# Attention with head mixing and a two-matrix MLP on one core: MLP products in runs of four, w_in spread over 48 steps, and both half-precision copies of e on ScalarE

## The chip, the cores and the metric

The kernel runs on one core of a Trainium2 chip. The metric is device time in microseconds, the median of three runs; the kernel before takes 851.1 us (850.71 to 854.3). The rows below come from one profiled execution, which took 852.55 us and whose span from the first to the last instruction is 850.8 us.

## The reference

Four batches, twelve heads, 448 positions, 64 channels per head. The scores are mixed across heads before the softmax, the probabilities are mixed across heads after it, and an MLP with a clipped gate follows:

```
scores = scale * q @ k.T                       # (4, 12, 448, 448)
scores = einsum('bhij,hg->bgij', scores, w_pre)
attn   = exp(scores - max) / sum
attn   = einsum('bhij,hg->bgij', attn, w_post)
x      = (attn @ v) as (1792 tokens, 768)
h      = x @ w_in                               # (1792, 2048), w_in is float64
out    = (h * clip(h + 3, 0, 6) / 6) @ w_out    # (1792, 768), w_out is float64
```

## The kernel before, in words

**Attention.** Each batch is cut into four chunks of query rows (120, 120, 120 and 90). For a chunk TensorE makes the scores of twelve heads in six products of two heads (L370). They go into the one two-bank PSUM tile `pair`, ScalarE copies them out (L402, tile `s`) and a DMA writes them to a scratch tensor `sd` in DRAM. When a whole chunk is in the scratch, it is read back in another layout, heads and ten query rows on the partitions: that is the load `T_all<-sd` (L453). One load serves two steps of ten rows each, called a step pair here; a batch has 45 steps and the whole attention 92 step pairs. Of each step pair TensorE mixes the heads (L461), VectorE takes the row maximum (L468), ScalarE the exponential `e` with its sum (L469), GpSimd multiplies with the reciprocal sum (L477). From step 24 on, `e` is split into two half-precision parts: `eh`, a rounded copy, and `el`, the rest, which GpSimd subtracts (L483). The copy of the first half of the step pair is made by ScalarE (L482), that of the second half by VectorE (L480). TensorE then mixes the heads again (L499) into `A`, which ScalarE and VectorE copy out of PSUM (L510, L508). After a chunk TensorE multiplies `A` with `v` (L536) into `x`.

**MLP, first part.** Two chunks make a group G of 240 or 208 tokens; there are eight groups. `moe1(G, fcs)` makes 18 matrix products for each of the 16 pieces `fc` of w_in (L694), in one PSUM bank each, ScalarE forms the gate (L703, tile `rl`), VectorE the product (L705, tile `g`, two pieces in one tile, two tiles in a ring), and a DMA writes two pieces to DRAM (L708). A piece of 18 products is called an MLP product below.

**w_in.** Each of its 16 pieces (786 KB of float64) is loaded (L622), decoded by ScalarE and VectorE (L582 to L597), scaled and split in two half-precision parts (L640 to L647). Two pieces are loaded before the first T load, the next six with steps 0, 2, ... 10, the last eight with steps 20, 23, ... 41. Groups that are ready before step 44 do their first eight pieces first; the other eight wait until step 44.

**MLP, second part.** The same with w_out, from 628 us to the end (L883).

**Order.** All operations are first put in a list with a modelled duration, dependencies and a priority (class `Plan`). `Plan.run` then walks through time and writes each engine's order out; TensorE takes the ready operation with the best priority, but stays with the kind of operation that it did last (`mode`) where one of that kind has a priority within `STAY`. MLP products have the worst priorities (5000 and more) and fill TensorE when nothing of the attention is ready in the model. In model gaps a `filler` puts products that no result needs (L729). All DMAs are issued by SP, in the order of the list. On the chip each engine runs its list in order and waits where the model was too early.

Of the kernel before, what the change touches and what calls it, by code (L numbers as in the profile page):

```python
# [42 lines left out]
LEAD = 7  # L43
HALF, W_AT, EARLY, V_AT = 8, 20, 2, 2
POST16 = 24
# [5 lines left out]
class Op:  # L51
    __slots__ = ("eng", "dur", "fn", "prio", "n", "succ", "order", "ready", "end", "bytes", "no", "mode", "takes")

# [48 lines left out]
class Plan:  # L102

    DMA_RATE = 330e3
    HOP = 0.14
# [7 lines left out]
    def op(self, eng, dur, fn, r=(), w=(), prio=0.0, after=(), nbytes=0, mode=0):  # L115
        o = Op()
        o.eng, o.dur, o.fn, o.prio, o.bytes, o.mode = eng, dur, fn, prio, nbytes, mode
        o.succ, o.order, o.n, o.ready, o.no, o.end, o.takes = [], [], 0, 0.0, len(self.ops), None, []
        deps = {}
# [30 lines left out]
    def run(self):  # L150
# [9 lines left out]
        free, wait, ready, out = {}, {}, {}, []  # L160
        bw, mode = 0.0, None

# [27 lines left out]
        while True:  # L190
# [19 lines left out]
            if e == "PE":  # L210
                at = [(avail(x[2]), x) for x in ready[e]]
                at = [x for z, x in at if z is not None and z <= t + 1e-9]
                x = min(at)
                x = min([z for z in at if z[2].mode == mode and z[0] < x[0] + self.STAY] or [x])
                ready[e].remove(x)
                o = x[2]
                for b in o.takes:
                    b.pool.take(b, self.HOP)
            else:
                while wait[e] and wait[e][0][0] <= t + 1e-9:  # L220
                    o = heapq.heappop(wait[e])[2]
                    heapq.heappush(ready[e], (o.prio, o.no, o))
                o = heapq.heappop(ready[e])[2]
# [24 lines left out]
def body(ctx: ExitStack, tc: tile.TileContext, q4, kT, vj, wpre0, wpost0, ident0, w_in, w_out, outT):  # L248
# [107 lines left out]

    def queries(b, c, at):
        t = buf(rot, [P, 6, CI], F32, "qx", f"qx_{b}_{c}", 2)
        qs[b, c] = t
        dma(P * 2880, lambda: SP.dma_start(t(), q4[b, c]), [], [t], at)  # L360

# [12 lines left out]
    def first_scores(pr, at):  # L374
# [8 lines left out]
        pe(0.73, products(q, k, pr, at2), [(k, pr % 3), q], ps, at, mode=1)  # L383
        h = 2 * pr
# [7 lines left out]
    def scores(b, c, pr, at):  # L392
# [6 lines left out]
        ps = place(pairs)  # L399
        pe(0.73, products(q, k, pr, [lambda u=u: ps()[:, u, :S] for u in range(2)]), [(k, pr % 3), q], [ps], at, mode=1)  # L400
        st = buf(rot, [CI, 2, S], F32, "s", f"s_{b}_{c}_{pr}", 2)
# [37 lines left out]
    def step(s):  # L439
# [24 lines left out]
        e = buf(rot, [P, 2, S], F32, "e", f"e_{s}", 3)  # L464
        pe(0.37 * R, pre, [T, wpre8], [*ps, (e, "pe")], s - 0.7, mode=1)
        eh, el = (buf(rot, [P, 2, S], F16, x, f"{x}_{s}", 2) if s >= POST16 else None for x in ("eh", "el"))
# [9 lines left out]
        for r in range(R):  # L476
            pool(0.63, lambda r=r: POOL.tensor_scalar(e()[:, r], e()[:, r], rr()[:, r:r + 1], 1.0, op0=ALU.mult, op1=ALU.mult), [rr], [(e, r)], s + 0.6 + 0.3 * r)  # L477
            if s >= POST16:
                if r:
                    dve(0.35, lambda: DVE.tensor_copy(eh()[:, 1], e()[:, 1]), [(e, 1)], [(eh, 1)], s + 0.95)  # L480
                else:
                    act(0.47, lambda: ACT.activation(eh()[:, 0], e()[:, 0], AF.Copy), [(e, 0)], [(eh, 0)], s + 0.65)  # L482
                pool(1.02, lambda r=r: POOL.tensor_tensor(el()[:, r], e()[:, r], eh()[:, r], op=ALU.subtract), [(e, r), (eh, r)], [(el, r)], s + 0.7 + 0.3 * r)  # L483
        if s < POST16:
            mix, dur = [(e, wpost_n)], 1.05
        else:
            mix, dur = [(eh, wpost_h), (eh, wpost_l), (el, wpost_h)], 0.4
        po = [place(mixed) for u in range(2)]
# [124 lines left out]
    def w_in_item(fc, after=()):  # L613
# [3 lines left out]
        w = wi_g[g]  # L617
        at = (fc - 4 if fc < EARLY else 2 * fc if fc < HALF else W_AT + 3 * (fc - HALF)) + 8
        raw = buf(rot, [P, NCC * P], I64, "stw", f"wi_{fc}", 2)
        o = buf(rot, [P, DM], F32, "wf", f"wf_i{fc}", 3)  # L620
        st, am1, t, r = (buf(rot, [P, 1], F32, f"wi_{x}", f"wi{x}_{fc}", 4) for x in ("st", "am", "t", "r"))
        dma(786432, lambda: SP.dma_start(raw(), w_in[fc]), [], [raw], at, after)  # L622
        rest = decode(raw, o, DM, (st, st), at, (0.81, 0.94, 0.48, 0.89, 0.89))
        slot, top = across(st, f"wi{fc}", at + 0.15)
        rest()
        p = (pwi, fc)

        dve(1.1, lambda: pow64(top, am1, t, lambda: pwi()[:, fc:fc + 1], r), [(slot, 1)], [am1, t, p, r], at + 0.2)

# [48 lines left out]
    def moe1(G, fcs):  # L678
# [7 lines left out]
        for fc in fcs:  # L686
# [16 lines left out]
            act(0.44, lambda fc=fc, pv=pv, r=r: ACT.activation(r()[:, :n], pv(), AF.Relu, bias=three()[:, fc:fc + 1], scale=uh()[:, fc:fc + 1]),  # L703
                [ps, (three, fc), (uh, fc)], [r], -80)
            dve(0.37, lambda fc=fc, pv=pv, r=r, gt=gt: DVE.scalar_tensor_tensor(gt()[:, fc % 2, :n], r()[:, :n], six()[:, fc:fc + 1], pv(),  # L705
                                                                                op0=ALU.min, op1=ALU.mult), [r, ps, (six, fc)], [(gt, fc % 2)], -80)
            if fc % 2:
# [7 lines left out]
    pool(2.0, lambda: POOL.memset(T_all()[:4], 0.0), [], [T_all], -20)  # L715
    warm = wpool.tile([P, 512], F16, tag="g", name="warm", bufs=2)
    DVE.memset(warm, 0.0)
# [31 lines left out]
    held, scales = [], []  # L749
# [194 lines left out]
```

## Time and profile before

| | |
|---|---|
| median of three runs | 851.1 us (850.71 to 854.3) |
| profiled execution, its own time | 852.55 us |
| its span | 850.8 us |
| TensorE busy | 816.4 us (96%) |
| VectorE, ScalarE, GpSimd busy | 547.1, 505.3, 371.6 us |
| mean granted TensorE clock | 0.984 |
| DMA | 177.09 MB, 208 GB/s over the span |

The busy share of TensorE is an average over very different stages: the start (to about 100 us), the attention with MLP products in between (to 547 us), the rest of the first MLP part (to 628 us) and the second MLP part. A row of a table of stretches gives its bounds and length in us, then busy time and number of instructions of each engine, then the granted clock, the busy share of the DMA engines and GB/s.

### The profile page before, as it was taken

The page shows a single profiled execution, that of the slowest core. Times are in us where ns is not written, and L with a number is a line of the kernel's source. Part 1 is how long each engine was busy: PE and PEld are TensorE (multiplying, and loading weights), DVE is VectorE, ACT ScalarE, POOL GpSimd, SP SyncE. Part 2 cuts the span into 40 slices and gives each one's busy share as a digit, 9 for nine tenths or more (in the row PEclk, how much of TensorE's full clock was granted, in tenths as well). Part 3 has the DMA queues.
Part 4 walks back from the last instruction along what each step waited for, and adds up shares of the span by engine and source line. Part 5 has one row for each costly group of instructions (what it writes and reads, how often), then busy time and mean ns, then how long its engine had stood idle before and what let it go on. Part 6 is the DMA issues. An engine that isn't in the chain of part 4 may idle for free.

```text
span 850.8 us, 25699 instructions
## 1 busy us (share of the span) xinstructions
PE 816.4 (96%) x10722; PEld 553.8 (65%) x10722; DVE 547.1 (64%) x1137; ACT 505.3 (59%) x969; POOL 371.6 (44%) x550
## 2 busy tenths in 40 slices
PE   8889998899999989999999999999999999999998
PEld 2456666567777656766766888999975555555554
DVE  5579799998667687876886665762228885333330
ACT  4547778678777867787667565753335454334330
POOL 1335879988868757877658656000000000000000
PEclk9969799999999999999999999999999999999999
DMA  9988978788697997987887622852247775545530
GB/s 317 308 254 264 288 237 261 216 243 249 193 255 220 280 286 239 278 262 234 247 262 231 202 76 80 248 183 69 67 143 222 245 216 156 175 145 163 160 121 33
DMA packets 82872, 177.09 MB, mean 208 GB/s; under 512 B 7604, under 2 KB 51732, under 8 KB 82756
## 3 DMA queue, kind: packets, MB, share of 16 engines
q1 hardware_dynamic: 82756, 175.45, 67.2%
q8 instruction: 84, 1.38, 0.7%
q14 instruction: 32, 0.26, 0.1%
HBM read 113.38 MB, written 62.04 MB: 206 GB/s over the span
## 4 chain that ended last, share of the span: by engine, by line
PE 73%; DVE 8%; DMA 7%; POOL 6%; ACT 3%; issue 2%; SPq 0%; ACTq 0%; DVEq 0%; POOLq 0%
PE single L883 26%; PE single L694 22%; PE single L499 7%; PE single L536 6%; PE pair L370 6%; PE single L461 5%; DMA sd<-s 3%; POOL el L483 2%; POOL e L477 2%; DVE nb L468 2%; DMA T_all<-sd 2%; DMA wo<-in_w_out 1%; ACT e L469 1%; ACT s L402 1%; DMA v<-in_vj 1%
## 5 line engine op out<-in xcount | busy, mean ns | idle before, releaser
L694 PEld LDWEIGHTS <-wi 128*128 128x128 f16 x2304 | 211.4, 98 | 37.4 <-issue 30.3
L694 PE MATMUL single<-x,wi 128*128 128x208 f16 (+1 forms) x2304 | 234.2, 260 | 1.6 <-DVE g L705 1.0
L883 PE MATMUL single<-g,wo 128*128 128x448 f16 x1152 | 219.1, 353 | 0.0
L483 POOL TENSOR_TENSOR el<-e,eh 128x448 f16<-128x448 f32 x156 | 167.5, 1087 | 44.5 <-ACT eh L482 30.4
L883 PEld LDWEIGHTS <-wo 128*128 128x128 f16 x1152 | 112.2, 98 | 104.2
L469 ACT ACTIVATE e<-single,nb 128x448 f32<-128x448 f32 x180 | 112.7, 632 | 48.0 <-DVE nb L468 44.3
L477 POOL TENSOR_SCALAR e<-e,r 128x448 f32<-128x448 f32 x180 | 124.9, 705 | 25.6 <-DVE r L472 23.2
L870 DVE SCALAR_TENSOR_TENSOR g<-gr,gs,g 128x896 f16<-128x896 f32 x64 | 73.4, 1151 | 85.8 <-ACT g L869 85.6
L468 DVE TENSOR_REDUCE nb<-single 128x1 f32<-128x448 f32 x180 | 103.3, 612 | 15.9 <-PE single L461 15.6
L705 DVE SCALAR_TENSOR_TENSOR g<-rl,six,single 128x240 f32<-128x240 f32 (+1 forms) x128 | 56.7, 443 | 77.0 <-ACT rl L703 74.5
L703 ACT ACTIVATE rl<-single,three,uh 128x240 f32<-128x240 f32 (+1 forms) x128 | 68.7, 537 | 61.6 <-PE single L694 60.2
L869 ACT ACTIVATE g<-gr,gs 128x896 f16<-128x896 f32 x64 | 66.2, 1037 | 63.8 <-DMA gr<-gd 62.2
L370 PE MATMUL pair<-ks,qx 64*64 64x448 f32 (+1 forms) x736 | 94.3, 579 | 6.1 <-ACT s L402 5.3
L402 ACT ACTIVATE s<-pair 120x896 f32<-120x896 f32 (+1 forms) x90 | 82.4, 915 | 26.7 <-PE pair L370 13.4
L461 PE MATMUL single<-T_all,wpre 64*64 64x448 f32 (+1 forms) x720 | 89.2, 560 | 6.4 <-DMA T_all<-sd 6.4
L876 POOL TENSOR_TENSOR us<-gu,wo_p 128x1 f32<-128x1 f32 x24 | 6.7, 313 | 174.7 <-DVE wo_p L606 142.5
L536 PE MATMUL single<-A,v 128*64 128x120 f32 (+1 forms) x1536 | 77.4, 261 | 3.7 <-DVE A L508 1.7
L499 PEld LDWEIGHTS <-eh 60*128 60x128 f16 x2496 | 66.4, 100 | 21.7 <-issue 19.4
L536 PEld LDWEIGHTS single<-A,v 128*64 128x64 f32 x1536 | 74.3, 137 | 9.4 <-issue 3.1
L499 PE MATMUL single<-wpost_h,el 60*128 60x60 f16 x1248 | 73.6, 202 | 2.5 <-POOL el L483 2.5
L499 PE MATMUL single<-wpost_h,eh 60*128 60x60 f16 x1248 | 73.6, 202 | 2.3 <-DVE A L508 2.0
L499 PE MATMUL single<-wpost_l,eh 60*128 60x60 f16 x1248 | 73.4, 202 | 0.8 <-issue 0.8
(116 smaller groups left out, 890.6 us busy)
## 6 DMA issues: line engine op xcount, KB each, us to landing
T_all<-sd SPq DMA_DIRECT2D x88, 420.0 KB, 5.9
sd<-s SPq DMA_DIRECT2D x72, 420.0 KB, 5.7
gr<-gd SPq DMA_DIRECT2D x64, 448.0 KB, 3.7
wi<-in_w_in SPq DMA_DIRECT2D x16, 768.0 KB, 6.6
wo<-in_w_out SPq DMA_DIRECT2D x24, 512.0 KB, 5.1
gd<-g SPq DMA_DIRECT2D x32, 240.0 KB, 3.1
sd<-s SPq DMA_DIRECT2D x24, 315.0 KB, 4.8
gd<-g SPq DMA_DIRECT2D x32, 208.0 KB, 2.6
```

The costliest lines, as they stand in the source:

```text
L370: PE.matmul(at[u]()[c:c + m], q()[r, pr, c:c + m], k()[r, pr % 3, :], start=True, stop=True)
L402: act(0.82, lambda: ACT.activation(st()[:n], ps()[:n, :, :S], AF.Copy), [ps], [st], at + 0.5)
L461: PE.matmul(ps[r]()[64 * u:64 * u + 64, :S], wpre8()[rows], T_all()[rows, slot, u], start=True, stop=True)
L468: dve(0.53, lambda r=r: DVE.tensor_reduce(nb()[:, r:r + 1], ps[r]()[:, :S], axis=AX.X, op=ALU.max, negate=True), [ps[r]], [(nb, r)], s + 0 ...
L469: act(0.62, lambda r=r: ACT.activation(e()[:, r], ps[r]()[:, :S], AF.Exp, bias=nb()[:, r:r + 1], accum_out=sm()[:, r:r + 1]), [ps[r], (nb, ...
L477: pool(0.63, lambda r=r: POOL.tensor_scalar(e()[:, r], e()[:, r], rr()[:, r:r + 1], 1.0, op0=ALU.mult, op1=ALU.mult), [rr], [(e, r)], s + ...
L483: pool(1.02, lambda r=r: POOL.tensor_tensor(el()[:, r], e()[:, r], eh()[:, r], op=ALU.subtract), [(e, r), (eh, r)], [(el, r)], s + 0.7 + 0 ...
L499: PE.matmul(out, x()[rows, r, js], z()[rows], start=(i == 0), stop=(i == len(mix) - 1))
L536: PE.matmul(ps()[u * D:(u + 1) * D, k:k + n], v()[:, jc, g * D:(g + 1) * D], a()[:, jc * H + g, :n], start=(jc == 0), stop=(jc == NJ - 1))
L694: PE.matmul(pv(), wi_g[g]()[:, w, f0, cc, :], x()[:, z, cc, :n], start=(cc == 0 and i == 0), stop=(cc == 5 and i == 2))
L870: dve(1.1, lambda: DVE.scalar_tensor_tensor(g()[:, 1], raw(), sb(), g()[:, 0], op0=ALU.mult, op1=ALU.subtract), [raw, sb, (g, 0)], [(g, 1) ...
L883: PE.matmul(ps()[:, :S], two()[:, z, w, fc, :], gs[h, b, k]()[:, x, fc % 2, :], start=(fc == 0 and i == 0), stop=(fc == NFC - 1 and i == 2))
```

## The change

The first half of the edits concerns the list: `Op` gets a field `then`, and TensorE, where the operation that it did last names a successor that is ready, takes this one ahead of anything else. `moe1` links pieces so that runs of up to four MLP products come about (0 to 3, 4 to 7, and so on). The gate now overwrites the place of `g` in its tile, the tile `rl` is gone, and the ring of `g` has three tiles in place of two; in the list the MLP product waits for its `g` tile. The last eight pieces of w_in are loaded with steps 20, 26, ... 62 in place of 20, 23, ... 41, and the MLP products of held groups are added two pieces at a time. One piece in place of two is loaded ahead of the first T load. The queries of chunk 1 come after the first T load, and its scores have a lead of 5 steps in place of 7. Both `eh` copies are ScalarE's. Some modelled durations and the modelled DMA rate are changed.

```diff
-HALF, W_AT, EARLY, V_AT = 8, 20, 2, 2
+HALF, W_AT, W_BY, EARLY, V_AT = 8, 20, 6, 1, 2
-    DMA_RATE = 330e3
+    DMA_RATE = 345e3
-                x = min([z for z in at if z[2].mode == mode and z[0] < x[0] + self.STAY] or [x])
+                x = min([z for z in at if z[2] is then] or [z for z in at if z[2].mode == mode and z[0] < x[0] + self.STAY] or [x])
+                then = x[2].then
-    def queries(b, c, at):
+    def queries(b, c, at, after=()):
...
-                if r:
-                    dve(0.35, lambda: DVE.tensor_copy(eh()[:, 1], e()[:, 1]), [(e, 1)], [(eh, 1)], s + 0.95)
-                else:
-                    act(0.47, lambda: ACT.activation(eh()[:, 0], e()[:, 0], AF.Copy), [(e, 0)], [(eh, 0)], s + 0.65)
+                act(0.47, lambda r=r: ACT.activation(eh()[:, r], e()[:, r], AF.Copy), [(e, r)], [(eh, r)], s + 0.65 + 0.3 * r)
...
-        at = (fc - 4 if fc < EARLY else 2 * fc if fc < HALF else W_AT + 3 * (fc - HALF)) + 8
+        at = (fc - 4 if fc < EARLY else 2 * fc if fc < HALF else W_AT + W_BY * (fc - HALF)) + 8
...
-                gt = buf(wpool, [P, 2, 240], F32, "g", f"g_{G}_{fc}", 2)
-            r = buf(wpool, [P, 240], F32, "rl", f"rl_{G}_{fc}", 2)
+                gt = buf(wpool, [P, 2, 240], F32, "g", f"g_{G}_{fc}", 3)
+            r = lambda gt=gt, fc=fc: gt()[:, fc % 2, :n]
-            pe(0.0077 * n, mm, [x, (uh, fc), *[(wi_g[g], (k, fc)) for k in range(3)]], [ps], at + fc)
+            m1 = pe(0.00775 * n, mm, [x, (uh, fc), *[(wi_g[g], (k, fc)) for k in range(3)]],
+               [ps, (gt, ("pe", fc % 2))], at + fc)
+            if fc % 4 and fc > fcs[0]:
+                m0.then = m1
+            m0 = m1
...
-            todo.append((prev + (pr * n) / 6 - LEAD, 0, b, c, pr))
+            todo.append((prev + (pr * n) / 6 - (LEAD if C > 1 else 5), 0, b, c, pr))
...
+        if s < NS:
+            step(s)
         while todo and todo[0][0] - 2 <= s:
             at, _, b, c, pr = todo.pop(0)
+            C0 = 4 * b + c - 1
             if pr == 0:
-                queries(b, c, at - 5)
+                queries(b, c, at - 5, [t_load[0]] if C0 == 0 else [])
             scores(b, c, pr, at)
-        if s < NS:
-            step(s)
...
-        if s in range(W_AT, W_AT + 3 * (NFC - HALF), 3):
-            w_in_item(HALF + (s - W_AT) // 3, [t_load[s]])
-        if s == W_AT + 3 * (NFC - HALF):
-            for G in held:
-                moe1(G, range(HALF, NFC))
+        if s in range(W_AT, W_AT + W_BY * (NFC - HALF), W_BY):
+            fc = HALF + (s - W_AT) // W_BY
+            w_in_item(fc, [t_load[s]])
+            if fc % 2:
+                n_wi = fc + 1
+                for G in held:
+                    moe1(G, range(fc - 1, fc + 1))
...
-                    late = s < W_AT + 3 * (NFC - HALF)
-                    moe1(2 * b + c // 2, range(HALF if late else NFC))
-                    held.extend([2 * b + c // 2] * late)
+                    moe1(2 * b + c // 2, range(n_wi))
+                    if n_wi < NFC:
+                        held.append(2 * b + c // 2)
```

## Rows read from the trace of the kernel before

**Rows 1.** Span and mean granted TensorE clock of the core.
```profile
core 0: 850.8 us, clock 0.984
```

**Rows 2.** Stretches: bounds, length, PE, PEld, DVE, ACT, POOL busy, clock, DMA, GB/s.
```profile
24.00:48.00 24.00, 17.70 (x188) 9.18 (x186) 13.01 (x26) 12.96 (x29) 6.99 (x13) 1.00 0.95 310
48.00:62.00 14.00, 13.95 (x99) 8.62 (x99) 9.11 (x21) 7.96 (x14) 7.26 (x13) 0.51 0.83 243
62.00:100.00 38.00, 35.76 (x426) 23.71 (x424) 31.87 (x84) 28.85 (x55) 24.43 (x44) 0.87 0.84 265
100.00:200.00 100.00, 90.05 (x1519) 63.79 (x1518) 95.96 (x200) 77.51 (x152) 85.17 (x125) 1.00 0.81 242
200.00:420.00 220.00, 214.46 (x4218) 152.73 (x4219) 162.37 (x358) 166.47 (x368) 166.57 (x228) 1.00 0.83 250
...
440.00:547.00 107.00, 106.28 (x1910) 85.58 (x1909) 69.03 (x148) 69.37 (x152) 62.82 (x87) 1.00 0.56 166
547.00:628.00 81.00, 81.00 (x862) 79.07 (x861) 32.77 (x70) 33.74 (x60) 0.47 (x3) 1.00 0.36 114
628.00:848.00 220.00, 219.11 (x1157) 112.44 (x1155) 102.03 (x150) 86.11 (x105) 4.38 (x12) 1.00 0.54 167
```

**Rows 3.** ScalarE's eh copies (L482) by stretch, one for each step pair: busy, clock, DMA.
```profile
100.00:200.00 100.00, 8.64 (x15) 1.00 0.81 242
200.00:300.00 100.00, 12.70 (x22) 1.00 0.80 238
```

**Rows 4.** VectorE's groups of lines, 100 to 200 us: busy us, mean ns | idle before.
```profile
L597 DVE SCALAR_TENSOR_TENSOR wf_i<-wi,wf_i 128x768 int32<-128x768 int32 x8 | 11.1, 1382 | 0.1
L593 DVE SCALAR_TENSOR_TENSOR wf_i<-wi,wf_i 128x768 int32<-128x768 int32 x8 | 10.8, 1356 | 0.1
L480 DVE CAST eh<-e 128x448 f16<-128x448 f32 x14 | 9.8, 698 | 1.0 <-POOL e L477 0.9
```

**Rows 5.** The two eh copies, whole span: ns min/median/max, first and last start.
```profile
L480 DVE CAST eh<-e x76: 371/394/1221, 103.7 to 522.2; 128x448 f16<-128x448 f32 x76
...
L482 ACT ACTIVATE eh<-e x80: 559/577/607, 102.8 to 525.4; 128x448 f16<-128x448 f32 x80
```

**Rows 6.** Waits of all engines: us in total, times, longest us.
```profile
POOL el L483 <- ACT eh L482: 30.4, 40, 10.1
...
PE single L461 <- DMA T_all<-sd: 6.4, 3, 3.8
...
PE pair L370 <- ACT s L402: 5.3, 10, 1.5
...
PE single L499 <- POOL el L483: 2.5, 3, 1.0
```

**Rows 7.** Chain that ended last: start us, us, what.
```profile
34.77 13.14 DMA T_all<-sd
...
188.54 1.95 PE single L694 x18
191.40 3.80 PE single L694 x36
...
528.23 9.33 PE single L694 x90
...
556.44 71.36 PE single L694 x756
```

**Rows 8.** Timeline of TensorE, its first MLP product: start us, us.
```profile
111.88 2.00 PE L694 MATMUL single<-x,wi 128*128 128x240 f16 x18
```

**Rows 9.** DMA issues by SP at the start: start us, us of issuing.
```profile
5.91 1.26 SPq L622 DMA_DIRECT2D wi<-in_w_in  x2
...
10.63 0.40 SPq L403 DMA_DIRECT2D sd<-s  x1
...
16.37 4.60 SPq L403 DMA_DIRECT2D sd<-s  x2
24.84 1.31 SPq L453 DMA_DIRECT2D T_all<-sd  x3
```

More of the change, by code (lines that the diff above doesn't have):

```diff
@@ L51 @@
 class Op:
-    __slots__ = ("eng", "dur", "fn", "prio", "n", "succ", "order", "ready", "end", "bytes", "no", "mode", "takes")
+    __slots__ = ("eng", "dur", "fn", "prio", "n", "succ", "order", "ready", "end", "bytes", "no", "mode", "takes", "then")
 class Buf:
@@ L117, in op @@
         o.eng, o.dur, o.fn, o.prio, o.bytes, o.mode = eng, dur, fn, prio, nbytes, mode
-        o.succ, o.order, o.n, o.ready, o.no, o.end, o.takes = [], [], 0, 0.0, len(self.ops), None, []
+        o.succ, o.order, o.n, o.ready, o.no, o.end, o.takes, o.then = [], [], 0, 0.0, len(self.ops), None, [], None
         deps = {}
@@ L160, in run @@
         free, wait, ready, out = {}, {}, {}, []
-        bw, mode = 0.0, None
+        bw, mode, then = 0.0, None, None
         def push(o):
@@ L355, in keys @@
                     b * STEPS - 30 + 3 * j + i if b else -14 + 3 * j + i)
-    def queries(b, c, at):
+    def queries(b, c, at, after=()):
         t = buf(rot, [P, 6, CI], F32, "qx", f"qx_{b}_{c}", 2)
         qs[b, c] = t
-        dma(P * 2880, lambda: SP.dma_start(t(), q4[b, c]), [], [t], at)
+        dma(P * 2880, lambda: SP.dma_start(t(), q4[b, c]), [], [t], at, after)
     S0 = buf(apool, [CI, H, S], F32, "A", "s0", 2)
@@ L382, in first_scores @@
             at2 = [lambda u=u: two()[:, u, :S] for u in range(2)]
-        pe(0.73, products(q, k, pr, at2), [(k, pr % 3), q], ps, at, mode=1)
+        pe(0.77, products(q, k, pr, at2), [(k, pr % 3), q], ps, at, mode=1)
         h = 2 * pr
@@ L399, in scores @@
         ps = place(pairs)
-        pe(0.73, products(q, k, pr, [lambda u=u: ps()[:, u, :S] for u in range(2)]), [(k, pr % 3), q], [ps], at, mode=1)
+        pe(0.77, products(q, k, pr, [lambda u=u: ps()[:, u, :S] for u in range(2)]), [(k, pr % 3), q], [ps], at, mode=1)
         st = buf(rot, [CI, 2, S], F32, "s", f"s_{b}_{c}_{pr}", 2)
@@ L464, in step @@
         e = buf(rot, [P, 2, S], F32, "e", f"e_{s}", 3)
-        pe(0.37 * R, pre, [T, wpre8], [*ps, (e, "pe")], s - 0.7, mode=1)
+        pe(0.39 * R, pre, [T, wpre8], [*ps, (e, "pe")], s - 0.7, mode=1)
         eh, el = (buf(rot, [P, 2, S], F16, x, f"{x}_{s}", 2) if s >= POST16 else None for x in ("eh", "el"))
@@ L486, in step @@
         else:
-            mix, dur = [(eh, wpost_h), (eh, wpost_l), (el, wpost_h)], 0.4
+            mix, dur = [(eh, wpost_h), (eh, wpost_l), (el, wpost_h)], 0.44
         po = [place(mixed) for u in range(2)]
@@ L622, in w_in_item @@
         dma(786432, lambda: SP.dma_start(raw(), w_in[fc]), [], [raw], at, after)
-        rest = decode(raw, o, DM, (st, st), at, (0.81, 0.94, 0.48, 0.89, 0.89))
+        rest = decode(raw, o, DM, (st, st), at, (0.81, 0.94, 0.5, 1.15, 1.25))
         slot, top = across(st, f"wi{fc}", at + 0.15)
@@ L626, in w_in_item @@
         p = (pwi, fc)
-        dve(1.1, lambda: pow64(top, am1, t, lambda: pwi()[:, fc:fc + 1], r), [(slot, 1)], [am1, t, p, r], at + 0.2)
+        dve(1.2, lambda: pow64(top, am1, t, lambda: pwi()[:, fc:fc + 1], r), [(slot, 1)], [am1, t, p, r], at + 0.2)
         def m4():
@@ L697, in moe1 @@
             if fc % 2 == 0:
-                gt = buf(wpool, [P, 2, 240], F32, "g", f"g_{G}_{fc}", 2)
-            r = buf(wpool, [P, 240], F32, "rl", f"rl_{G}_{fc}", 2)
+                gt = buf(wpool, [P, 2, 240], F32, "g", f"g_{G}_{fc}", 3)
+            r = lambda gt=gt, fc=fc: gt()[:, fc % 2, :n]
             if gi == 0 and b == 0:
                 pool(0.25, lambda fc=fc: POOL.tensor_tensor(uh()[:, fc:fc + 1], pw2()[:, fc:fc + 1], u1(), op=ALU.mult), [(pw2, fc), u1], [(uh, fc)], -90)
-            pe(0.0077 * n, mm, [x, (uh, fc), *[(wi_g[g], (k, fc)) for k in range(3)]], [ps], at + fc)
[L703 to L706, printed above, removed]
+            m1 = pe(0.00775 * n, mm, [x, (uh, fc), *[(wi_g[g], (k, fc)) for k in range(3)]],
[3 more added lines that the diff above has]
+            m0 = m1
+            act(0.44, lambda fc=fc, pv=pv, r=r: ACT.activation(r(), pv(), AF.Relu, bias=three()[:, fc:fc + 1], scale=uh()[:, fc:fc + 1]),
+                [ps, (three, fc), (uh, fc)], [(gt, fc % 2)], -80)
+            dve(0.37, lambda fc=fc, pv=pv, r=r: DVE.scalar_tensor_tensor(r(), r(), six()[:, fc:fc + 1], pv(),
+                                                                                op0=ALU.min, op1=ALU.mult), [ps, (six, fc)], [(gt, fc % 2)], -80)
             if fc % 2:
@@ L715, in body @@
     pool(2.0, lambda: POOL.memset(T_all()[:4], 0.0), [], [T_all], -20)
-    warm = wpool.tile([P, 512], F16, tag="g", name="warm", bufs=2)
+    warm = wpool.tile([P, 512], F16, tag="g", name="warm", bufs=3)
     DVE.memset(warm, 0.0)
@@ L746, in body @@
         for pr in range(6):
-            todo.append((prev + (pr * n) / 6 - LEAD, 0, b, c, pr))
+            todo.append((prev + (pr * n) / 6 - (LEAD if C > 1 else 5), 0, b, c, pr))
     todo.sort()
-    held, scales = [], []
+    held, scales, n_wi = [], [], HALF
     for s in range(NS + 12):
```

## The prediction

> **What bounds the kernel now.** First the clock and the span [rows 1]: at 0.984 over 850.8 us about 13.6 us of the span are lost to TensorE's lower level. Then the table of stretches [rows 2]. From 547 us TensorE is busy to within 1 us of every stretch: 81 us of MLP products, then the second MLP part, 220 us. Nothing in the change shortens those products, so the end comes as early as TensorE gets through the rest of its work. Before 547 us it is idle 6.3 us in 24 to 48, 2.2 us in 62 to 100, 10 us in 100 to 200, and then 5.5 us in 220 (2.5 per 100). TensorE is therefore the bound from 200 us on, and the reader should see that another engine is it in 100 to 200: VectorE is busy 95.96 us of 100 there, against 74% in 200 to 420. The count of step pairs says the same: 15 in 100 to 200 and 22 in the next 100 us [rows 3]. VectorE's groups of lines of that stretch [rows 4] show what it does in excess: eight w_in pieces, of which two lines alone take 21.9 us, and the casts of eh with 9.8 us.
>
> At the start the DMA engines are the bound: share 0.95 at 310 GB/s in 24 to 48 [rows 2], and a T load issued at 34.77 lands 13.14 us later [rows 7]. TensorE's wait for T loads is 6.4 us in all, 3.8 us at the longest [rows 6]. Right behind that landing, from 48 to 62 us, the granted clock is 0.51, the level of 1.2 GHz [rows 2]; 0.49 x 14 = 6.9 us go there, and 0.13 x 38 = 4.9 us in 62 to 100.
>
> The sum goes against the profiled execution, 852.55 us (span 850.8 and 1.75 around it); it is 1.45 us above the median 851.1, which is taken off at the end.
>
> **Runs of four.** A single MLP product of 240 tokens costs 1.95 us of the chain, two in a row 3.80, five in a row 9.33 [rows 7]: a run costs 0.10 us more than its products. Between the first, at 111.88 [rows 8], and the last run of 42 products (x756 at 556.44 [rows 7]) TensorE's timeline has, the first counted, 68 runs with 86 products, 56 of them of one. With links of up to four, and the two held groups in smaller bits, groups 0 and 1 make 11 runs and the other 54 products 13 or 14: some 43 runs fewer. Each missing run also joins what stood on its two sides, which the trace does not price by itself; the nearest rows are again the 0.10 us of a run, so one saving of 0.10 is the lower end (4.3 us) and three of it the upper (13 us). I take 0.14, near the priced row: **-6 us**. While a run of four, some 7.5 us, is on, attention products wait behind it on TensorE, and ScalarE, VectorE and GpSimd work off what they have; this costs nothing as long as MLP products remain, and 42 of them still do when the attention is over. The third g tile and the missing rl change no count of instructions; their stalls were small, I cost them at 0.
>
> **w_in over 48 steps, casts off VectorE.** Half of the eight pieces leave the stretch 100 to 200 and take at least 11 us with them by the two lines, the casts 9.8 more: VectorE goes from 96 to 75 us for the same 15 step pairs. What is late next is GpSimd: 166.57 us in 220 [rows 2] at 22 step pairs per 100 us is 3.4 us a pair, so it allows some 20 in that stretch and TensorE can be filled as it is behind 200. The idle time would go from 9.95 to 2.5 us per 100, -7.4; the four pieces that move come to lie where VectorE has 26% of its time free. Ends: 0 (the waits go over to GpSimd whole) and -9.95. I take **-6 us**, nearer the row of the next stretch.
>
> The cast on VectorE takes 371 ns at best, 394 in the median and 1221 at worst, while ScalarE's stays between 559 and 607 [rows 5]. The Trainium skill says why (SBUF — State Buffer, section Who interferes with whom): a cast can run in a mode that takes the port pair which VectorE shares with GpSimd, and whoever starts second is blocked for the other's whole instruction; ScalarE has its own ports. The spread of the rows agrees. By the rows alone only VectorE's time comes back; by the rule GpSimd gets back what it loses behind casts as well, and the term would be the full -7.4.
>
> **Both casts on ScalarE.** 76 copies of 577 ns, 43.9 us more for ScalarE. In 200 to 420 it is busy 166.47 us; with 46 step pairs it gets 26.5 us more, 193 of 220 or 88%: not the bound, but fuller. GpSimd already waits 30.4 us for the 80 copies that ScalarE makes, 0.38 us each, and TensorE waits 2.5 us for GpSimd's el [rows 6], a twelfth of it. The second copies would add 29 us of GpSimd's waits, and a twelfth, 2.4 us, is the near value; score copies (L402) also queue behind them on ScalarE, which alone frees `pair` and on which TensorE waits 5.3 us now; I let this grow by two fifths, 2.1. **+4.5 us**; ends 0 and +29 (no MLP product covers any wait).
>
> **The start.** A w_in piece of 786 KB at 310 GB/s is 2.5 us ahead of the first T load (two pieces at 5.91, the T loads at 24.84 [rows 9]). The queries of chunk 1 and the three score writes of it that are issued by 16.37 (430 KB, 1.4 us each) also move behind that load, which then might be 8 to 9 us earlier; but all of them must still be through before the T load of step 12, on DMA engines without room, and so they only change places. On SP the order of these issues changes, not their number. **-2.5 us**; ends 0 and -9.
>
> **The clock.** If the T loads come 2.5 us earlier, the 3.8 us wait at 48 is mostly gone and with it the lower level behind it. The order of the whole start is new, though, and a wait of the same kind may stand elsewhere. Ends: the whole 11.8 us of the two stretches back, or 7 more lost. **-3 us**. The changed durations and the modelled DMA rate only reorder; at 0, with the range for it.
>
> Sum: -6 - 6 + 4.5 - 2.5 - 3 = -13, 839.5 us; against the median **838 us**.
>
> **Rivals.** *GpSimd takes VectorE's place* (0.17). For it: GpSimd is busy 85% in 100 to 200. Against: it holds 22 pairs per 100 us at 76% later. Then the second term is 0, start and clock give 1, runs -6, ScalarE +4.5: 851.1 - 2.5 = 849 us.
>
> *ScalarE's queue decides* (0.15), the other side. Each second eh stands in ScalarE's order between exponentials and score copies, and `pair` is one tile: scores come late, T loads behind them on SP too, and TensorE stands before products (L499 on el, L370 on pair) that the list took to be ready. For it: 0.38 us wait per copy today. Against: TensorE's own waits are 2.5 and 5.3 us. It decides from the point where more than 0.23 us of each copy reaches TensorE (17.5 us, the gains above); at 0.35 us of 76, 26.6 us, the time is 851.1 - 17.5 + 26.6 = 860 us.
>
> *The start and its clock gain whole* (0.12): the first T load 7 us earlier is passed on, idle time from 100 to 200 and the lower level go: -7 - 9 - 8 - 7 + 3 = -28, 823 us.
>
> That the runs don't come about, because linked products lack a PSUM bank or a g tile in the list, is part of the first rival: 6 us less, 844.
>
> **Numbers.** Forecast 0.56 (828 to 846), GpSimd 0.17, ScalarE 0.15, the large gain 0.12. Half a per cent, 4.3 us, is what can be told from no change. Faster: 0.56 + 0.12, less a little for its upper edge and with the runs' failure, 0.69; same 0.17; slower 0.14. The range 825 to 853 leaves out half of the large gain and most of ScalarE's case.
>
> **What would show it.** In the stretches: VectorE near 75 in 100 to 200 and TensorE's idle time there under 4 us; 17 or more step pairs. In TensorE's timeline: some 25 runs before the long one, mostly x72. In the waits: GpSimd el on ScalarE eh near 60 us, TensorE's wait for el and for `pair` not above 15 together. The first T load issued before 22 us. The forecast is wrong if ScalarE is above 92% busy from 200 to 420 with TensorE idle over 10 us there, or if a stretch of clock 0.5 longer than 14 us stands in the first 100 us.

## The result, and the profile after

The changed kernel takes 845.07 us (median of 20 runs, 835.16 to 853.76), the kernel before 853.62 us (20 runs beside it, 850.2 to 857.26): so 8.6 us less by the medians. The ratio 0.9881 [0.9858, 0.9903], 10 us, leaves out the five executions of the changed kernel above 847 us, which count as slow. The profiled execution took 843.31 us, 9.2 us less than that of before. The forecast of 838 was 7 us low, and 845.07 lies inside its own range of 828 to 846.

Core of the changed kernel, span and mean granted clock, against [rows 1]:

```profile
core 0: 841.5 us, clock 0.984
```

The stretches of the changed kernel, columns as in [rows 2] (length, then PE, PEld, DVE, ACT and POOL busy, granted clock, DMA share, GB/s):

```profile
24.00:48.00 24.00, 19.32 (x199) 10.79 (x197) 16.72 (x32) 14.72 (x33) 7.97 (x16) 0.85 1.00 315
48.00:62.00 14.00, 13.35 (x108) 9.34 (x106) 7.95 (x25) 4.38 (x6) 2.54 (x5) 0.50 0.42 123
62.00:100.00 38.00, 32.72 (x385) 19.31 (x377) 31.80 (x76) 29.07 (x52) 25.14 (x46) 0.92 0.94 294
100.00:200.00 100.00, 95.99 (x1611) 70.38 (x1610) 80.98 (x181) 85.52 (x177) 79.52 (x120) 1.00 0.84 256
200.00:420.00 220.00, 216.02 (x3992) 164.50 (x3991) 140.40 (x311) 175.95 (x381) 145.63 (x212) 1.00 0.76 230
440.00:547.00 107.00, 102.64 (x1978) 80.72 (x1980) 71.74 (x158) 78.99 (x175) 72.64 (x103) 1.00 0.67 197
547.00:628.00 81.00, 80.32 (x977) 72.09 (x970) 42.45 (x81) 44.04 (x80) 9.66 (x16) 1.00 0.52 168
628.00:848.00 220.00, 209.84 (x1108) 107.65 (x1106) 99.63 (x147) 83.55 (x102) 4.39 (x12) 1.00 0.51 160
```

From 100 to 200 us VectorE falls from 95.96 to 80.98 us and TensorE's idle time from 9.95 to 4.01. From 200 to 420 the idle time hardly changes (5.54 to 3.98), and from 440 to 547 it rises (0.72 to 4.36). Idle time alone therefore doesn't explain 10 us. I also summed, from the single records of TensorE, its work at the price that each kind of product has in an unbroken row: from 200 to 400 us before holds 181.5 us of such work and after 187.6. Of the 6.1 us, 1.5 is idle time and 4.6 is time around changes from one kind of product to another: 13.8 us with 149 stretches of one kind before, 9.2 us with 104 after, some 0.09 us a change in both (0.12 if an unbroken row is priced by the spacing of its starts alone, so this figure is an estimate).

By the same sum, the table says how far ahead of the kernel before (us of work done) the changed kernel is at a moment:

| at us | 60 | 80 | 100 | 180 | 280 | 320 | 440 | 547 | 640 |
|---|---|---|---|---|---|---|---|---|---|
| ahead | -1.7 | -5.7 | -3.3 | +3.9 | +1.4 | +6.8 | +11.8 | +9.7 | +9.3 |

The start loses, 100 to 180 and 280 to 440 gain, and 180 to 280 and 440 to 547 give some 2 us back each. The entries hang on those prices and are good to 1 or 2 us; the last one is the difference of the spans (850.8 - 841.5).

The waits of the changed kernel, against [rows 6] (us in total, times, longest):

```profile
POOL el L481 <- ACT eh L480: 43.8, 39, 5.1
...
PE pair L371 <- ACT s L403: 6.2, 9, 2.8
...
PE single L462 <- DMA T_all<-sd: 2.9, 4, 0.9
```

The chain that ended last of the changed kernel, its MLP products of the first part (start, us, what), against [rows 7]:

```profile
133.74 7.49 PE single L692 x72
...
208.01 6.53 PE single L692 x72
...
603.04 16.05 PE single L692 x180
```

x72 is a run of four: 7.49 us at 240 tokens, where four singles of 1.95 would be 7.80. In TensorE's whole timeline there are 30 MLP runs before the last attention product (576.5 us), 23 of them of four, against 66, mostly of one, in the kernel before. Behind the last attention product 24 MLP products of this part remain, where before 48 remained behind 546 us.

SP's issues of the changed kernel at the start (start, us of issuing), against [rows 9]:

```profile
19.21 1.31 SPq L454 DMA_DIRECT2D T_all<-sd  x3
...
31.55 0.33 SPq L404 DMA_DIRECT2D sd<-s  x1
...
44.01 8.42 SPq L404 DMA_DIRECT2D sd<-s  x3
...
61.12 3.20 SPq L404 DMA_DIRECT2D sd<-s  x2
...
65.49 0.52 SPq L454 DMA_DIRECT2D T_all<-sd  x1
```

The first T load is issued 5.6 us earlier, and the T load of step 12 at 65.49 instead of 49.08: between the two stand the six score writes of chunk 1, which come from 31.55 on. Meanwhile the DMA engines have little to do (share 0.42 from 48 to 62 us, 0.83 before). The granted clock by tens of us, of the changed kernel:

```profile
40.00:50.00 10.00, 7.19 (x53) 4.40 (x53) 5.83 (x12) 5.80 (x13) 2.86 (x6) 0.71 0.85 301
50.00:60.00 10.00, 10.00 (x83) 7.31 (x76) 5.85 (x13) 2.84 (x4) 2.10 (x2) 0.50 0.39 122
60.00:70.00 10.00, 9.35 (x125) 6.70 (x125) 6.74 (x26) 7.85 (x10) 6.32 (x16) 0.77 0.75 230
```

That is 5.8, 10 and 4.6 us at the lower level (clock 0.50, 1.2 GHz), one stretch of 20.4 us from 44.1 to 64.6. Before, the stretch from 48 us on is 13.7 us long [rows 2]. In both it begins right behind a wait of TensorE: there the 3.8 us for a T load [rows 6], here the longest wait for `pair`, 2.8 us, which ends at 44.0. Over the whole span the lower level costs the same in the two profiled executions (clock 0.984 in both).

### The profile page after: what moved, and what is told of

Same layout as the page of the kernel before. It is cut to its first block, busy times and chain, and to the rows that moved or that the text cites. A ratio compares the mean times of both kernels' runs of the same rounds, so it can differ in the third digit from the quotient of the medians.

```text
span 841.5 us, 25708 instructions
## 1 busy us (share of the span) xinstructions
PE 810.2 (96%) x10732; PEld 556.9 (66%) x10732; DVE 513.3 (61%) x1061; ACT 537.4 (64%) x1045; POOL 361.8 (43%) x550
## 4 chain that ended last, share of the span: by engine, by line
PE 72%; DMA 12%; DVE 6%; ACT 4%; POOL 3%; issue 2%; SPq 1%; ACTq 0%; POOLq 0%
PE single L888 26%; PE single L692 20%; PE single L497 8%; PE single L534 7%; PE pair L371 6%; PE single L462 5%; DMA T_all<-sd 3%; DMA wo<-in_w_out 2%; DMA sd<-s 2%; DMA wi<-in_w_in 2%; DMA v<-in_vj 2%; ACT s L403 2%; DVE nb L469 1%; ACT e L470 1%; POOL e L478 1%
## 5 line engine op out<-in xcount | busy, mean ns | idle before, releaser
L692 PE MATMUL single<-x,wi 128*128 128x208 f16 (+1 forms) x2304 | 226.8, 259 | 3.1 <-DVE g L707 1.8
L692 PEld LDWEIGHTS <-wi 128*128 128x128 f16 x2304 | 213.2, 98 | 20.1 <-issue 13.8
L481 POOL TENSOR_TENSOR el<-e,eh 128x448 f16<-128x448 f32 x156 | 166.8, 1088 | 45.7 <-ACT eh L480 43.8
L478 POOL TENSOR_SCALAR e<-e,r 128x448 f32<-128x448 f32 x180 | 121.9, 688 | 41.0 <-DVE r L473 38.9
L705 ACT ACTIVATE g<-single,three,uh 128x240 f32<-128x240 f32 (+1 forms) x128 | 68.8, 539 | 52.8 <-PE single L692 51.1
L371 PE MATMUL pair<-ks,qx 64*64 64x448 f32 x736 | 94.5, 585 | 6.5 <-ACT s L403 6.2
L707 DVE SCALAR_TENSOR_TENSOR g<-g,six,single 128x240 f32<-128x240 f32 (+1 forms) x128 | 56.5, 443 | 71.6 <-ACT g L705 69.5
L480 ACT ACTIVATE eh<-e 128x448 f16<-128x448 f32 x156 | 86.5, 577 | 8.7 <-POOL e L478 8.3
L462 PE MATMUL single<-T_all,wpre 64*64 64x448 f32 (+1 forms) x720 | 84.7, 548 | 3.2 <-DMA T_all<-sd 2.9
L534 PEld LDWEIGHTS single<-A,v 128*64 128x64 f32 x1536 | 74.8, 138 | 10.6 <-ACT e L470 3.9
```

The lines of the kernel that those rows point to most:

```text
L371: PE.matmul(at[u]()[c:c + m], q()[r, pr, c:c + m], k()[r, pr % 3, :], start=True, stop=True)
L462: PE.matmul(ps[r]()[64 * u:64 * u + 64, :S], wpre8()[rows], T_all()[rows, slot, u], start=True, stop=True)
L480: act(0.47, lambda r=r: ACT.activation(eh()[:, r], e()[:, r], AF.Copy), [(e, r)], [(eh, r)], s + 0.65 + 0.3 * r)
L534: PE.matmul(ps()[u * D:(u + 1) * D, k:k + n], v()[:, jc, g * D:(g + 1) * D], a()[:, jc * H + g, :n], start=(jc == 0), stop=(jc == NJ - 1))
L692: PE.matmul(pv(), wi_g[g]()[:, w, f0, cc, :], x()[:, z, cc, :n], start=(cc == 0 and i == 0), stop=(cc == 5 and i == 2))
```

## Experiments

The theory at this point: the gain comes from the runs (fewer changes of kind) and from VectorE's relief between 100 and 200 us, while the start costs some 3 us. Rivals: one part alone makes the whole gain, the runs are worth nothing, or the new durations in the list's model do it by reordering. "before + x" below is the kernel before with one part of the change, "after - x" the changed kernel with one part undone. Ratios are against the kernel before, run beside it (its medians were about 853 to 854 us).

**after - runs**, `u1_no_runs`

```diff
-                m0.then = m1
+                pass
```

> The changed kernel with the links between MLP products taken out, all else kept. Theory (each run costs some 0.14 us more than its products, and about 43 runs are saved): the time rises by 6 us, to about 851 (4 to 10 us), and TensorE's timeline has 60 or more runs before the long one at the end. Rival (the gain is VectorE's relief alone, the runs are neutral because TensorE's idle time is filled anyway): within 2 us of 845.

Measured: 861.07 us, 1.0101 [1.0054, 1.0149]. Without the links the changed kernel is slower than the kernel before: in the changed kernel they are worth 16 us by the medians, far more than the -6 of the forecast and than the theory's 4 to 10. Stretches of this kernel:

```profile
100.00:200.00 100.00, 93.55 (x1609) 62.77 (x1608) 82.31 (x182) 86.23 (x182) 84.13 (x121) 1.00 0.84 261
200.00:420.00 220.00, 210.83 (x3801) 144.98 (x3800) 140.73 (x313) 180.77 (x397) 158.49 (x227) 0.98 0.81 243
```

From 100 to 547 us TensorE is idle 18.5 us, 12.8 in the changed kernel. It changes its kind of product some 74 times more, 7 us at 0.09. Its clock of 0.98 from 200 to 420, where the changed kernel has 1.00, costs some 4 us. By this estimate the changes of kind are less than half of what the links are worth here; the rest is waits and the lower level.

**after - order of the start**, `u2_chunk1_early`

```diff
-            todo.append((prev + (pr * n) / 6 - (LEAD if C > 1 else 5), 0, b, c, pr))
+            todo.append((prev + (pr * n) / 6 - LEAD, 0, b, c, pr))
...
-                queries(b, c, at - 5, [t_load[0]] if C0 == 0 else [])
+                queries(b, c, at - 5, [])
```

> The changed kernel with the queries of chunk 1 loaded at the start again and its scores at a lead of 7 steps; one w_in piece ahead of the first T load is kept. Theory (the late scores of chunk 1 hold back the T load of step 12, which the changed kernel issues at 65.5 us in place of 49.1, and this costs the start 3 to 6 us): faster than the changed kernel by 3 to 6 us, 839 to 842, T load of step 12 issued before 55 us. Rival (the earlier first T load is worth as much as the later chunk costs, or the DMA engines are full either way): within 2 us of 845. Second rival (without the new order the first T load comes back to 25 us and the time is lost there): 848 or more.

Measured: 851.83 us, 0.9967 [0.9934, 0.9999]. With chunk 1 early again and one w_in piece ahead of T, the kernel loses most of its gain, against the theory, although the T load of step 12 is issued at 47.31 us, as the theory wanted. So having that load early is not enough for a faster kernel. The clock of its profiled execution (0.968 over the span) is the lowest of all twelve. Over the executions that enter the ratios, the median clock is 0.975, against 0.984 of the changed kernel: 0.009 of 850 us is 7.7 us, all of the difference between the two ratios (7.3 us). The stretch 100 to 200 of this kernel shows it too, with DMA, VectorE, ScalarE and GpSimd less busy than in the changed kernel:

```profile
100.00:200.00 100.00, 93.11 (x1479) 67.02 (x1477) 78.94 (x160) 79.08 (x162) 73.46 (x109) 0.92 0.75 226
```

So this mixed start is worse than that of the changed kernel, by the clock as far as the rows show. It doesn't say that the new start is better than the old one, which b3 tests.

**after - 48 steps**, `u3_w_by_3`

```diff
-HALF, W_AT, W_BY, EARLY, V_AT = 8, 20, 6, 1, 2
+HALF, W_AT, W_BY, EARLY, V_AT = 8, 20, 3, 1, 2
```

> The changed kernel with the last eight w_in pieces over 24 steps again (20, 23, ... 41). Theory (VectorE is the bound from 100 to 200 us through these pieces): the time rises by 3 to 6 us, to 848 to 851, VectorE above 90 of 100 us in 100 to 200 and TensorE idle over 6 us there. Rival (the casts were what filled VectorE, the pieces can stay): within 2 us of 845, VectorE below 90.

Measured: 845.74 us, 0.9912 [0.9879, 0.9946]. The intervals of this and of the changed kernel (0.9881) overlap: the spread of w_in over 48 steps is worth 1 us by the medians and 3 by the ratios, which is not told from nothing.

**after - second copy on ScalarE**, `u4_cast_vector`

```diff
-                act(0.47, lambda r=r: ACT.activation(eh()[:, r], e()[:, r], AF.Copy), [(e, r)], [(eh, r)], s + 0.65 + 0.3 * r)
+                if r:
+                    dve(0.35, lambda: DVE.tensor_copy(eh()[:, 1], e()[:, 1]), [(e, 1)], [(eh, 1)], s + 0.95)
+                else:
+                    act(0.47, lambda: ACT.activation(eh()[:, 0], e()[:, 0], AF.Copy), [(e, 0)], [(eh, 0)], s + 0.65)
```

> The changed kernel with the second copy of e on VectorE again. Theory (the casts cost VectorE 10 us of 100 in the stretch 100 to 200 and lock GpSimd out at times, but add nothing that TensorE waits for elsewhere): the time rises by 1 to 3 us, 846 to 848. Rival (ScalarE's fuller queue costs the changed kernel more than VectorE's relief gives): faster than 845 by 2 us or more. Second rival (the casts are half of the gain): 850 or more.

Measured: 849.02 us, 0.9934 [0.99, 0.9969]: the second copy on ScalarE is worth some 4 us in the changed kernel (the two intervals just touch), both sides taken together (the forecast had ScalarE's side at +4.5 and VectorE's relief in another term). Stretches of u3, and then of u4, show where:

```profile
100.00:200.00 100.00, 90.63 (x1497) 64.50 (x1496) 85.44 (x184) 83.65 (x163) 79.61 (x122) 1.00 0.81 250
```

```profile
100.00:200.00 100.00, 91.67 (x1561) 66.10 (x1555) 84.53 (x187) 74.71 (x150) 78.03 (x114) 0.99 0.79 248
200.00:420.00 220.00, 216.52 (x3908) 164.15 (x3903) 159.04 (x358) 160.42 (x346) 150.06 (x211) 1.00 0.74 228
```

Either half of VectorE's relief undone gives back most of the gain of 100 to 200 us (idle 9.4 and 8.3 us; 4.0 in the changed kernel, 9.95 before). By the end u3 has recovered it and u4 hasn't: its VectorE stays 19 us busier from 200 to 420 (159.04 against 140.40).

**before + runs**, `b1_runs_only`: the field `then`, the planner's preference for it, and

```diff
-            pe(0.0077 * n, mm, [x, (uh, fc), *[(wi_g[g], (k, fc)) for k in range(3)]], [ps], at + fc)
+            m1 = pe(0.0077 * n, mm, [x, (uh, fc), *[(wi_g[g], (k, fc)) for k in range(3)]], [ps], at + fc)
+            if fc % 4 and fc > fcs[0]:
+                m0.then = m1
+            m0 = m1
```

> The kernel before with the links between MLP products alone (two g tiles and rl kept). Taking the links out of the changed kernel cost 16 us. Theory (the gain is mostly the runs: fewer changes of kind on TensorE at some 0.09 us each, and attention products that pile up and no longer stall it): faster than before by 6 to 14 us, 839 to 847, with fewer than 110 segments of one kind on TensorE from 200 to 400 us in place of 149. Rival (the links only mend what the other edits spoil): within 3 us of 853.

Measured: 854.28 us, 1.0002 [0.9977, 1.0027]: alone the runs are worth nothing. They do come about: from 200 to 400 us 149 stretches of one kind become 97, and the time around changes 13.8 us becomes 9.9. By the sum of work the kernel is 5.8 us ahead at 520 us and 2.5 behind at 600. The rows of this kernel, 100 to 200 and then near the end of attention:

```profile
100.00:200.00 100.00, 89.29 (x1452) 63.87 (x1445) 87.75 (x185) 73.55 (x143) 82.48 (x119) 0.97 0.76 232
```

```profile
520.00:540.00 20.00, 18.32 (x305) 11.85 (x300) 13.30 (x28) 14.63 (x31) 12.66 (x17) 0.96 0.77 222
540.00:560.00 20.00, 20.00 (x389) 16.23 (x384) 13.23 (x28) 11.93 (x27) 13.12 (x18) 0.96 0.50 147
560.00:580.00 20.00, 20.00 (x372) 16.35 (x366) 12.54 (x33) 12.38 (x31) 13.71 (x22) 1.00 0.35 94
580.00:600.00 20.00, 19.37 (x329) 17.39 (x325) 9.49 (x20) 9.84 (x21) 8.30 (x12) 1.00 0.24 75
```

From 100 to 200 TensorE is as idle (10.7 us) as before, and its clock is 0.97. The MLP products are done earlier, so attention ends later, at 603 us instead of 546, with 16 products left instead of 48. From 547 us the kernel before runs MLP products without a break [rows 7]; here GpSimd is at work until 600 and TensorE goes on changing between kinds; from 520 to 600 it is idle for 2.3 us, and its clock is 0.96 from 520 to 560. What the runs earned in the middle is given back there.

**before + both copies on ScalarE**, `b2_copies_only` (the edit of u4, the other way round)

> The kernel before with both copies of e on ScalarE alone. Theory (without the runs TensorE waits for ScalarE's fuller queue: the changed kernel without links is 8 us over the kernel before): slower than before by 3 to 9 us, 856 to 862. Rival (VectorE's relief is worth 4 us here as in the changed kernel): 849 or less.

Measured: 845.96 us, 0.9921 [0.9893, 0.9949]. The theory is refuted: this one piece of the change gives most of it, 8.2 of 8.6 us by the medians and 6.7 of 10.2 by the ratios. Stretches and a wait of this kernel:

```profile
100.00:200.00 100.00, 95.84 (x1584) 67.02 (x1580) 88.03 (x190) 84.63 (x170) 83.95 (x129) 0.97 0.82 253
200.00:420.00 220.00, 215.23 (x4058) 153.54 (x4057) 133.42 (x295) 179.36 (x399) 150.38 (x216) 1.00 0.80 240
```

```profile
POOL el L480 <- ACT eh L479: 34.6, 40, 2.6
```

VectorE loses 7.9 us from 100 to 200 and TensorE's idle time goes from 9.95 to 4.16 (at a clock of 0.97, so up to 3 us of the busy time are the lower level's). GpSimd's wait for ScalarE hardly grows (30.4 to 34.6), and its wait for VectorE's cast (8.5 us before) goes.

**before + start**, `b3_start_only`: EARLY 1, the step ahead of the scores, chunk 1's queries behind the first T load, its lead 5

> The kernel before with the start of the changed kernel alone: one w_in piece ahead, queries of chunk 1 after the first T load, lead 5, step ahead of scores. Theory (the start changes places, not bytes, and what the clock does in it is by chance): within 4 us of 853. Rival (undoing two of these edits cost the changed kernel 7 us, so the start is a gain): 848 or less. Second rival (the T load of step 12 comes 16 us later in the changed kernel): 857 or more.

Measured: 857.32 us, 1.0043 [1.0014, 1.0073]. Alone the new start costs 3.7 us; the T load of step 12 is issued at 70.97 here. Two stretches of this kernel:

```profile
48.00:62.00 14.00, 14.00 (x114) 10.77 (x112) 9.75 (x20) 6.84 (x12) 6.21 (x11) 0.50 0.52 175
62.00:100.00 38.00, 34.97 (x332) 21.00 (x330) 28.59 (x69) 25.88 (x45) 20.10 (x39) 0.75 0.84 261
```

The lower level reaches further than before (0.75 against 0.87 from 62 to 100), and the DMA engines are half idle from 48 to 62, as in the changed kernel. This profiled execution took 862.59 us, 5 us above the median, so its clock shows the new start worse than it mostly is.

**before + runs + copies**, `c1_runs_copies` (the edits of b1 and b2)

> The kernel before with the links between MLP products and both copies of e on ScalarE, nothing else. Alone the links changed nothing and the copies gave 8 us. Theory (the links save changes of kind only as long as no other engine makes TensorE idle; VectorE did so from 100 to 200 us in the links-only kernel, and the copies lift that): the two add up to more than the copies alone, 836 to 843, TensorE idle in 100 to 200 under 6 us. Rival (the links are a mere reordering without a value of their own): 844 to 849. Second rival (with links the attention ends late and TensorE runs out of MLP products at the end): last attention product after 600 us and 850 or more.

Measured: 845.07 us, 0.9907 [0.9874, 0.994]: the same as the copies alone, and as the changed kernel (the ratios differ by 2 us, inside their intervals). The two don't add, and the theory is refuted. A stretch of this kernel:

```profile
100.00:200.00 100.00, 93.63 (x1553) 70.14 (x1553) 90.37 (x189) 82.77 (x166) 86.16 (x129) 1.00 0.82 251
```

TensorE is idle for 6.4 us there, 4.2 with the copies alone, and for 14.2 against 10.6 us from 100 to 547. Its changes of kind fall by 78 (7 us at 0.09), and its last attention product starts at 593 us instead of 541.

**after, with more to do for TensorE at the start**. Two kernels give it extra products without use (at least two ahead of every operation that the list places in a stretch, where a PSUM bank is free, 9 to 105 us in the first and 9 to 45 us in the second; 110 and 32 more than the changed kernel has).

```diff
+        keep = 9.0 <= t0 < 105.0
+        if keep:
+            n = max(n, 2)
-        if t0 < FILL_FROM or t0 > FILL_TO or n < 3 or not free:
+        if t0 < FILL_FROM or t0 > FILL_TO or n < (2 if keep else 3) or not free:
```

> The changed kernel with at least two products that no result needs (L731, 0.2 us each at 2.4 GHz) ahead of each operation of TensorE whose modelled start lies between 9 and 105 us, 110 more in all. Theory (the stretch at 1.2 GHz behind the waits of the start costs 3 to 6 us and changes from run to run; products in the gaps hold the clock up): mean clock 0.99 or more in the first 100 us' stretches, 838 to 842. Rival (the 110 products, some 25 us of TensorE, push the chain of the start back by more than the clock gives): 847 or more. Second rival (the DMA engines bound the start whatever the clock is): within 2 us of 845 with a higher clock.

Measured: 846.76 us, 0.9922 [0.9891, 0.9954]. Two stretches of this kernel:

```profile
24.00:48.00 24.00, 22.99 (x229) 10.91 (x227) 16.94 (x33) 15.03 (x34) 7.94 (x16) 1.00 0.97 306
...
62.00:100.00 38.00, 37.84 (x385) 18.32 (x383) 27.90 (x64) 27.55 (x51) 20.92 (x38) 1.00 0.89 268
```

The clock is 1.00 from 24 to 100 us, but TensorE has hardly any idle time left behind 62, and its work done by 100 us is 42.3 us against 43.8 of the changed kernel: the extra products cost what the clock gives. Hence the second one, `45.0` in place of `105.0`:

> The changed kernel with two products that no result needs ahead of each operation of TensorE whose modelled start lies between 9 and 45 us only (32 more in all). With 9 to 105 us the clock was 1.00 from 24 to 100 us, the time 847 and the work done by 100 us 1 us less. Theory (the products after 60 us cost what the clock gave): clock 0.95 or more in 48 to 62, 839 to 843. Rival (the start is bound by the order of its DMAs and not by TensorE's clock): 844 to 848 whatever the clock is.

Measured: 838.71 us (835.67 to 842.79), 0.9824 [0.9796, 0.9853], clock 0.997. This beats both kernels; its interval and that of the changed kernel (from 0.9858) don't meet. Stretches of this kernel:

```profile
24.00:48.00 24.00, 23.26 (x229) 10.91 (x227) 17.21 (x33) 15.24 (x34) 7.95 (x16) 1.00 0.96 308
48.00:62.00 14.00, 13.29 (x192) 9.45 (x193) 11.59 (x38) 9.40 (x14) 7.08 (x14) 1.00 0.70 220
62.00:100.00 38.00, 32.44 (x372) 17.91 (x370) 33.35 (x77) 30.28 (x58) 25.07 (x48) 0.96 0.97 320
```

From 48 to 62 TensorE is as long busy as in the changed kernel (13.29 and 13.35 us) but gets 192 products through instead of 108, and the DMA share is 0.70 instead of 0.42; the T load of step 12 is issued at 60.26 instead of 65.49. Work done by 100 us is 49.0 us, 5.2 more than in the changed kernel; at the end the spans of the two profiles differ by 4.4 us, the ratios by 5 us and the medians by 6.4. So what c2 gains, it has gained by 100 us.

**after with the modelled durations and DMA rate of before**, `c3_old_model`, for instance

```diff
-    DMA_RATE = 345e3
+    DMA_RATE = 330e3
...
-            mix, dur = [(eh, wpost_h), (eh, wpost_l), (el, wpost_h)], 0.44
+            mix, dur = [(eh, wpost_h), (eh, wpost_l), (el, wpost_h)], 0.4
```

> The changed kernel with the modelled durations and the modelled DMA rate of the kernel before. Theory (they only reorder, at 0): within 3 us of 845. Rival (the list of before thinks TensorE faster than it is, by 0.04 us for each of the score products and so on, and TensorE stands before operations that are not ready): 849 or more, with TensorE idle over 20 us from 100 to 547 us in place of 13.

Measured: 845.88 us, 0.9901 [0.9873, 0.9929]. The new numbers of the model are worth nothing that shows, as the theory had it.

**The same without the runs**, `d1_no_runs_old_model` (the edits of c3 and of u1). u1 and b1 disagree on what the runs are worth, 16 us and 0; this run asks whether u1 drew an unlucky order of the list.

> The changed kernel without the links and with the modelled durations and DMA rate of before, so a third order of the same work. Open is why the changed kernel without links took 861 us, 15 more than the kernel before with the copies alone (846) and 16 more than with links. Theory (the links hide what the remaining edits leave: with single products every one of such lists stands before attention products that are not ready): 856 or more again, TensorE idle over 17 us from 100 to 547 us. Rival (861 belongs to that one order, which loses 8 us between 240 and 280 us): 845 to 852.

Measured: 860.27 us, 1.0089 [1.006, 1.0117], as slow as u1 in another order of the list, and 14 us over c3, which has the links. Stretches of this kernel:

```profile
100.00:200.00 100.00, 89.03 (x1531) 57.87 (x1532) 79.05 (x178) 84.34 (x173) 81.20 (x122) 0.97 0.87 265
200.00:420.00 220.00, 211.06 (x3904) 149.69 (x3902) 138.80 (x312) 180.49 (x392) 157.95 (x228) 0.99 0.81 243
```

TensorE is idle 11.0 us and 8.9 us there, 4.0 and 4.0 in the changed kernel, although VectorE is as little busy as in that one. So the rest of the change (start, third g tile, no rl, w_in pieces, the two held groups in smaller bits) costs some 15 us beside the copies as long as MLP products come one at a time, and nearly nothing when they come in fours. Which piece of it costs that, no run here separates; it stays open.

## Why the prediction was right, and where its steps were not

**Total.** Forecast -13 us from the profiled time; measured -9.2 there, -8.6 by the medians and -10 by the ratio. Of the five terms, the one of w_in and the casts held, ScalarE's was too dear, the start's had the wrong sign, the clock's gain is not in the two profiles, and the one of the runs held only beside the other parts. That the sum still fits is in part luck: the errors cancel. By one of its own signs, a stretch of clock 0.5 longer than 14 us in the first 100, the forecast was wrong: that stretch is 20.4 us long.

**Runs of four, -6.** The price per change came out near the estimate: from 100 to 547 us there are 291 stretches of one kind before and 221 after, and 70 x 0.09 = 6.3 us; the runs before the last attention product fell by 36, not 43. What failed is the view that such a price can be added: the runs alone are worth 0 (b1), on top of the copies 0 (c1 against b2), and in the changed kernel 14 to 16 (d1 against c3, u1). "This costs nothing as long as MLP products remain" was the wrong step: they are the work that covers waits, and b1 shows that using them up sooner lets attention end later (603 us instead of 546), with TensorE changing kinds to the end.

**w_in over 48 steps and casts off VectorE, -6.** The size was right for its stretch: idle time 9.95 to 4.01, and 7.2 us of lead from 100 to 180 us, of which 2.5 are lost again by 280. VectorE's share of it was smaller than worked out (81 us instead of 75), and there are no more step pairs. ScalarE's eh copies of the changed kernel, two for a pair (busy, clock, DMA; one for a pair in [rows 3]):

```profile
100.00:200.00 100.00, 17.57 (x31) 1.00 0.84 256
200.00:300.00 100.00, 19.38 (x35) 1.00 0.76 222
```

These are 15.5 and 17.5 pairs, against 15 and 22: the time went to MLP products, which the planner now places earlier, not to attention as I had it. Over the whole kernel the source is the casts (b2: 7 to 8 us, u4: 4) rather than the w_in pieces (u3: 1 to 3, not told from nothing). Of the port rule (the Trainium skill, SBUF — State Buffer, section Who interferes with whom) the spread of VectorE's cast [rows 5] agrees with VectorE's side; on GpSimd's side its subtraction for el takes 1087 ns in the mean before, from 100 to 547 us, and 1090 after, its scaling of e 699 and 679: some 3 us over 151 instructions, so most of what the rule would give back to GpSimd doesn't show.

**Both copies on ScalarE, +4.5.** Mis-sized. GpSimd's wait for eh is 43.8 us, not 60, TensorE's for `pair` 6.2 (5.3 before, forecast 7.4), and ScalarE is 80% busy from 200 to 420, not 88. b2 shows the step that failed: I doubled the wait for ScalarE's copies and left out that GpSimd's wait for VectorE's went.

**Start, -2.5.** Wrong in sign. The first T load was issued at 19.21, before 22 as said, but 3.3 us of lead are lost by 100 us, and b3 puts the start at +3.7. I had seen that the pieces "only change places"; the step that failed is to have followed the first T load alone. The T load behind chunk 1's score writes moved from 49.08 to 65.49. That this load by itself costs the time is not shown: u2 has it at 47.31 and is slower, at a lower clock.

**Clock, -3.** TensorE's wait for T loads fell as forecast (6.4 to 2.9 us, the longest 0.9), but the lower level didn't go with it: "a wait of the same kind" stood elsewhere, 2.8 us for `pair`, and the stretch behind it grew from 13.7 to 20.4 us. Other stretches at the lower level became shorter, so the term is 0 in the two profiles (clock 0.984 in both); the medians over the executions that enter the ratios (0.984, against 0.979 to 0.982 of the kernel before, run beside the experiments) would make it some 2 to 4 us won, and no run tells how much of that is the new start's. That 32 products without use win 5 to 6 us here (c2) shows that the clock at the start, which I had priced at 11.8 us in all, was the larger thing to win.

**Rivals.** GpSimd in VectorE's place: no, it falls to 79.52 us from 100 to 200. ScalarE's queue: no, by the waits above. That the start gains whole: no. All three were rightly the less likely ones; that one part alone would bring most of it was none of them.

## What to carry to other kernels

Parts of a change to a hand-ordered list don't add: the links were worth 0, 0 and some 16 us in three surroundings, so price an edit together with what covers it, and measure it alone and undone. A saved switch on a full engine is a gain only if the work that is now done sooner was not what filled the gaps later. When a load is brought forward, follow the next load of the same buffer as well, and every wait of TensorE up to it: what was pushed behind the first load may stand in front of the next, and the wait that is cured may come back at another tile.

## What the runs showed of the hardware that was not expected

TensorE's clock at the start decides several microseconds, and differs from run to run of one kernel: of the changed kernel's runs, spans were 833.4 us at a mean clock of 0.993, 839.2 at 0.990 and 841.5 at 0.984. Between the first and the last of these the time lost to the lower level grows from 5.8 to 13.5 us, by about as much as the span. u1 has the same order of TensorE's instructions up to u1's first MLP product, at 112 us, and yet its rows at the start are others than those of the changed kernel above:

```profile
24.00:48.00 24.00, 22.51 (x186) 11.73 (x184) 14.90 (x28) 13.22 (x30) 6.50 (x13) 0.72 0.99 311
48.00:62.00 14.00, 13.29 (x195) 9.65 (x193) 12.77 (x40) 9.65 (x15) 6.96 (x15) 1.00 0.63 203
```

Here the lower level (1.2 GHz, half of the full 2.4) lies in 24 to 48 and is over by 48, and u1 is 3.3 us ahead of the changed kernel between 80 and 100 us. A single profile of a start can therefore mislead by that much; a median of several executions is safer.
